# The spectral filter's products move from GpSimd to VectorE, its loads are split and issued earlier, and the planner counts the array's work differently

## The chip, the cores and the metric

The kernel runs on one core of a Trainium2 chip. The metric is the device time of one execution in microseconds. Before the change four runs took 985.72, 997.27, 997.92 and 1008.8 us; their median is 997.59 us.

## The reference

Two independent operations on 2048 x 640 inputs in bf16, whose results lie side by side in the output:

```python
# A: a spectral filter
X = jnp.fft.rfft2(x.astype(jnp.float32))       # 2048 x 321, complex
y = jnp.fft.irfft2(X * (w_r + 1j * w_i), s=(2048, 640))
# B: softmax attention, 32 heads of width 20
scores = jnp.einsum("bhqd,bhkd->bhqk", q, k) * 20 ** -0.5
o = jnp.einsum("bhqk,bhkd->bhqd", jax.nn.softmax(scores), v)
out = jnp.concatenate([y, o_merged @ wo], axis=-1)
```

## The kernel before

A planner written in Python (class `FK`) runs through an imagined execution once, at build time. It keeps a clock `self.now`, gives every operation an assumed duration, and whenever an engine would be free it picks that engine's next instruction (`dispatch`, L2188). The result is a fixed order for each of the five engines. On the chip every engine works through its list strictly in that order and waits on semaphores where data or a buffer is not ready. An instruction that has to wait holds up everything behind it on its engine. SP's list holds the DMA issues. If the imagined durations are wrong, the order stays as planned and the waits appear in the run.

*Attention.* The queries are cut into 4 blocks of 512, the heads into 8 groups of 4, which makes 32 units. A unit has 64 score tiles of 128 keys x 512 queries (16 key blocks x 4 heads). A score matmul (L1702) uses only 32 of the array's 128 rows, and up to four tiles run side by side; a PV matmul (L1884) uses 32 of the 128 columns, again four at once. ScalarE exponentiates groups of 3 and 2 tiles alternately from PSUM banks 0 to 2 and 3 to 4 (L1719). VectorE helps: it takes pairs of tiles, moves each out of PSUM (L1792) and computes the exponential in seven steps on SBUF (L1829 to L1842). At the end of a unit the sums are copied out (L1903), the denominators take a way over four small DMAs, a reciprocal (L1921), DRAM and back, and GpSimd normalizes (L1942). The output projection is L1964. Projections of keys (L1529), queries (L1605) and values (L1546, L1567) are jobs, as is everything of the filter.

*Jobs.* A `Job` is a list of matmuls into one of two PSUM banks (7 and 5) and an eviction `ev`, which any of the planner's rules may give to VectorE. The banks are shared with VectorE's score tiles. `try_bg_pe` (L2098) starts the job of the lowest priority number whose predecessors are done. Events are jobs without matmuls: they issue loads or GpSimd work and count as done after an assumed time, `lat` x 1200 ns for a load.

*The filter's stages*, as jobs with lowest precedence, one after the other:
- S2: the weights w_r and w_i are loaded (`s2_load`, L1085, two DMAs of 1284 KB), GpSimd rearranges them (`s2_relayout`, L1101), PE transposes them (L1116).
- S1: A_x is loaded (`s1_load`, L1136, one DMA of 2560 KB) and transposed (L1149). S3: DFT over columns (L1169). S4: the first factor of the DFT over rows (L1197), its constants in two loads (`s4_load`). S5: transposes (L1116).
- S6: the second factor (L1229): per chunk of 4 of 41 blocks of 128 columns two matmuls each for the real and the imaginary part, each evicted to SBUF (`XY`, by `copy_on`, L227). S7: GpSimd multiplies by the filter, six `tensor_tensor` instructions per chunk (L1258 to L1263): four products into four f32 tiles `tmp`, a difference and a sum into `XY`. The chunks go one after the other, 11 in all.
- S8 to S11: the inverse (L1229, L1116, L1297, L1323) with its constants (`s10_load`, `s11_load`).

Buffers of the stages lie over each other in zones A, B, C and K; keys such as `("z", "A", 1)` order a zone's next tenant behind the last one's readers.

*Order of the queue on PE.* `dispatch` for PE tries scores, a lone score tile for VectorE, PV, the tail, a job's next matmul, and last `warm()`, a dummy matmul (L1592). `share()` (L2169) is the planner's measure of how busy the array was over the last 2200 ns: `pe_dur` (L1634) enters every operation, 51 ns per tile for scores and PV, its duration otherwise, with 100 ns (`MODE`) where the kind of matmul changes. Dummies are placed while the share is not above `WARM_SHARE` = 0.46. Filter jobs that are ahead of a schedule, which spreads them over 680 us of planned time, are held back while the share is above it.

Of the kernel before, what the change touches and what calls it, by code (L numbers as in the profile page):

```python
# [244 lines left out]
class Job:  # L245
    def __init__(self, name, prio, pe, ev, after=(), minp=-10 ** 9, post=None, banks=None, cond=None, lat=0):
# [15 lines left out]
        self.ev_eng = None  # L262


class KB:
# [805 lines left out]
    def mk_jobs_A(self, p0_after):  # L1071
# [13 lines left out]
        def s2_load(J, p):  # L1085
            P = self.P
            wn = self.Wn
            P.add("pool", lambda e: e.memset(wn.rearrange("p c k l -> p (c k) l")[:, :, 321:328], 0.0),
                  w=zw("A", 1) + [("Wnpad",)], name="ms_wn")
            for c, src in ((0, self.A_w_r), (1, self.A_w_i)):  # L1090
                self.dma(wn[:, c, :, 0:321], src.rearrange("(kb ka) l -> ka kb l", ka=128), w=zw("A", 1) + [("Wn", c)], name="ld_W%d" % c)
            self.dma(self.kron.rearrange("p m k -> p (m k)"), self.c_kron.ap(), w=[("kron",)], name="ld_kron")
        J_s2l = evt("S2load", p0_after, s2_load, lat=8)

        J_s2r = {}
        for c in range(2):
# [6 lines left out]
            J_s2r[c] = evt("S2relayout%d" % c, [J_s2l] + ([J_s2r[0]] if c else []), s2_relayout, lat=(17 if c == 0 else 18))  # L1103
# [32 lines left out]
        def s1_load(J, p):  # L1136
            self.dma(self.xAn, self.A_x[0].rearrange("(sa sb) d -> sa sb d", sb=16), w=[("xAn",)] + zw("A", 2), name="ld_xA")
            self.dma(self.FD.rearrange("p c r l -> p (c r l)"), self.c_FD.ap(), w=[("FD",)], name="ld_FD")
        J_s1l = evt("S1load", [J_s2r[1]], s1_load, lat=8)
        st["S1"] = []  # L1140
        for dc in range(5):
            for hb in range(2):
                pe = []
                for i in range(8):
# [5 lines left out]
                    pe.append((mk, 60.0, [("xAn",), ("ident",), zr("A", 2)]))  # L1150
# [32 lines left out]
        J_s4l = evt("S4load", st["S3"], s4_load, lat=5)  # L1183
        st["S4"] = []
        for sbv in range(16):
            if sbv == 8:
                J_s4l = evt("S4load1", list(st["S4"]), lambda J, p: s4_load(J, p, 1), lat=5)
# [26 lines left out]
        def kron_jobs(tag, src, srckey, zrd, dst, dstkey, zwr, sign, after_of, stage):  # L1214
            out = {}
            for ci_, (b0, n) in enumerate(chunks):
                for co in range(2):
# [14 lines left out]
                    def mkev(bank, co=co, b0=b0, n=n):  # L1232
# [9 lines left out]
        s6 = kron_jobs("FS2_", self.BT, lambda c, ci_: ("BT", c, ci_ // 2), zr("A", 4), self.XY, lambda c, ci_: ("XY", c, ci_), zw("B", 4), +1,  # L1242
                       lambda ci_: [s5[(0, ci_ // 2)], s5[(1, ci_ // 2)]], st["S6"])
        s7 = {}
        kw = [("Wp", c, b) for c in range(2) for b in range(6)] + [zr("C", 1)]
        for ci_, (b0, n) in enumerate(chunks):
            def hook(J, p, ci_=ci_, b0=b0, n=n):
                P = self.P
                ne = n * 128
                xr = self.XY[:, 0, b0:b0 + n, :].rearrange("p b m -> p (b m)")  # L1250
                xi = self.XY[:, 1, b0:b0 + n, :].rearrange("p b m -> p (b m)")
                wr = self.Wp[:, 0, b0:b0 + n, :].rearrange("p b m -> p (b m)")
                wi = self.Wp[:, 1, b0:b0 + n, :].rearrange("p b m -> p (b m)")
                t = [tt[:, 0:ne] for tt in self.tmp]
                kx = [("XY", 0, ci_), ("XY", 1, ci_)]
                zb = [zr("B", 4)]
                tw = zw("K", 2)
                P.add("pool", lambda e: e.tensor_tensor(t[0], xr, wr, ALU.mult), r=[kx[0]] + kw + zb, w=[("tmp", 0)] + tw, name="pw")  # L1258
                P.add("pool", lambda e: e.tensor_tensor(t[1], xi, wi, ALU.mult), r=[kx[1]] + kw + zb, w=[("tmp", 1)] + tw, name="pw")
                P.add("pool", lambda e: e.tensor_tensor(t[2], xr, wi, ALU.mult), r=[kx[0]] + kw + zb, w=[("tmp", 2)] + tw, name="pw")  # L1260
                P.add("pool", lambda e: e.tensor_tensor(t[3], xi, wr, ALU.mult), r=[kx[1]] + kw + zb, w=[("tmp", 3)] + tw, name="pw")
                P.add("pool", lambda e: e.tensor_tensor(xr, t[0], t[1], ALU.subtract), r=[("tmp", 0), ("tmp", 1), zr("K", 2)], w=[kx[0]], name="pw")
                P.add("pool", lambda e: e.tensor_tensor(xi, t[2], t[3], ALU.add), r=[("tmp", 2), ("tmp", 3), zr("K", 2)], w=[kx[1]], name="pw")  # L1263
            lat = 3 + int(6 * n * 128 * 2.0 / T_PERIOD)
            aft = [s6[(ci_, 0)], s6[(ci_, 1)]] + ([s7[ci_ - 1]] if ci_ else st["S4"] + st["S2"])
            s7[ci_] = evt("S7_%d" % ci_, aft, hook, lat=lat)
# [14 lines left out]
        J_s10l = evt("S10load", [s7[nch - 1]], s10_load, lat=6)  # L1281
        st["S10"] = []
        for h in range(2):
            if h:
                J_s10l = evt("S10load1", list(st["S10"]), lambda J, p: s10_load(J, p, 1), lat=6)
# [85 lines left out]
class FK(KB):  # L1371
# [142 lines left out]
    def mk_jobs_B_static(self):  # L1514
# [5 lines left out]
        for g in range(NG):  # L1520
            for kc in range(4):
# [11 lines left out]
                if g:  # L1533
                    J.minp = 18500.0 + 1100.0 * g
        V = {}
# [98 lines left out]
    def pe_dur(self, dur, mode, tiles=0):  # L1634
        if mode != self.mode:
            dur += MODE
            self.mode = mode
        if self.now < 12000.0:
            dur *= 2.0
        self.pe_hist.append((self.now, 51.0 * tiles if tiles else dur))  # L1640
        self.wlog.append(self.pe_hist[-1])
# [435 lines left out]
    def run_events_jobs(self):  # L2077
        for J in [J for J in self.jobs if not J.pe]:
# [5 lines left out]
            if J.name.startswith("S2relayout"):  # L2084
                pool = 4600.0
            elif J.name.startswith("S7"):
                pool = 8200.0
# [279 lines left out]
```

## Time and profile before

| | before |
|---|---|
| median of 4 runs | 997.59 us |
| the profiled execution | 997.27 us, its span 995.5 us |
| PE, DVE, ACT, POOL busy | 878.4, 822.0, 848.4, 153.6 us |
| mean granted TensorE clock | 0.878 of full speed |
| ScalarE's exponentials (L1719) | 837.3 us, 724 instructions |
| VectorE's score evictions (L1792) | 163.3 us, 238 instructions of 686 ns |
| GpSimd's products (L1258 to L1263) | 66 instructions |
| dummies (L1592) | 126 |

The time lies in overlapping work of three engines, so the share of busy time says little. It is better read in stretches between two times of the span: how busy each engine was there, at which granted clock, and how many score tiles came out. The clock column is the mean of what the throttle granted in that stretch; 0.50 is half speed. A "[8.74 <-POOL arena L1101]" behind a line of the timeline means that the engine stood idle for 8.74 us before it, until that line on POOL released it. Durations of VectorE's instructions overlap their neighbours by some 0.08 us, so the distance between two starts is what one costs in a row.

### The profile page before, as it was taken

The numbers are of one execution on the slowest core, as the hardware profiler recorded it, in microseconds if no ns is written. First come the engines' busy times: TensorE is split into PE (matmuls) and PEld (weight loads), VectorE is DVE, ScalarE is ACT, GpSimd is POOL, SyncE is SP. The second block draws the span as 40 slices with busy tenths as digits, with TensorE's granted clock in tenths as the row PEclk, the third lists the DMA queues.
The fourth block names the chain that finished last, engine by engine and source line by source line (L and its number), as shares of the span: only waits on it lengthen the run. The fifth ranks groups of instructions, "written<-read, shape, count | busy, mean of one in ns | idle before, by whom it ended". The sixth has DMA issues, their size and how long they took to land.

```text
span 995.5 us, 15128 instructions
## 1 busy us (share of the span) xinstructions
PE 878.4 (88%) x6072; PEld 281.1 (28%) x6072; DVE 822.0 (83%) x1571; ACT 848.4 (85%) x744; POOL 153.6 (15%) x122
## 2 busy tenths in 40 slices
PE   8799989957999999898988878898899999898896
PEld 4333223212333332222312221332333333212212
DVE  5787999966779997879797989887899689989973
ACT  6689989975879998979968786898999899989974
POOL 4200000022000000000099653000000000010000
PEclk9899999997679998958859887797999999769959
DMA  7100000044000000110000000101101110100000
GB/s 209 34 13 12 12 6 8 12 121 151 2 19 32 13 12 12 44 33 12 13 12 15 24 13 6 50 12 54 52 12 39 39 33 33 39 12 12 12 12 29
DMA packets 31296, 31.75 MB, mean 32 GB/s; under 512 B 13300, under 2 KB 26356, under 8 KB 30836
## 3 DMA queue, kind: packets, MB, share of 16 engines
q1 hardware_dynamic: 31220, 30.73, 10.0%
q8 instruction: 49, 0.80, 0.4%
q14 instruction: 27, 0.22, 0.1%
HBM read 24.97 MB, written 5.50 MB: 31 GB/s over the span
## 4 chain that ended last, share of the span: by engine, by line
DVE 36%; PE 31%; ACT 15%; issue 7%; DMA 6%; SPq 4%; POOL 1%; ACTq 0%; POOLq 0%
ACT arena L1719 15%; PE ps L1702 10%; DVE arena L227 7%; PE ps L1884 7%; DVE arena L1792 6%; DMA arena<-arena 5%; SPq L360 4%; DVE arena L1837 4%; DVE arena L1833 3%; DVE arena L1840 3%; DVE arena L1835 3%; DVE arena L1829 3%; DVE arena L1831 2%; DVE arena L1842 2%; PE ps L1592 2%
## 5 line engine op out<-in xcount | busy, mean ns | idle before, releaser
L1719 ACT ACTIVATE arena<-ps 128x1536 bf16<-128x1536 f32 x724 | 837.3, 1261 | 125.0 <-PE ps L1702 83.5
L1702 PE MATMUL ps<-arena 32*128 32x512 bf16 x2048 | 334.9, 425 | 49.9 <-ACT arena L1719 37.6
L1884 PE MATMUL ps<-arena 128*32 128x512 bf16 (+1 forms) x2048 | 223.6, 430 | 9.4 <-DVE arena L1842 5.9
L1792 DVE TENSOR_SCALAR arena<-ps 128x512 uint16<-128x512 f32 x238 | 163.3, 686 | 46.1 <-PE ps L1702 45.2
L227 DVE CAST arena<-ps 128x320 bf16<-128x320 f32 (+5 forms) x284 | 160.8, 568 | 32.9 <-PE ps L1297 6.3
L1942 POOL TENSOR_TENSOR arena<-arena 128x512 bf16<-128x512 f32 x31 | 44.8, 1444 | 779.2 <-DMA arena<-rscr 773.2
L1702 PEld LDWEIGHTS ps<-arena 32*128 32x128 bf16 x2048 | 74.7, 92 | 271.8 <-ACT arena L1719 182.3
L1884 PEld LDWEIGHTS ps<-arena 128*32 128x32 bf16 (+1 forms) x2048 | 51.9, 93 | 152.5 <-issue 122.7
L1840 DVE TENSOR_TENSOR arena<-arena 128x1024 uint16<-128x1024 uint16 x119 | 89.3, 750 | 0.8
L1833 DVE TENSOR_TENSOR arena<-arena 128x1024 f16<-128x1024 f16 x119 | 87.1, 732 | 1.7
L1837 DVE TENSOR_TENSOR arena<-arena 128x1024 f16<-128x1024 f16 x119 | 86.7, 729 | 2.0
L1835 DVE TENSOR_SCALAR arena<-arena 128x1024 f16<-128x1024 f16 x119 | 59.8, 502 | 1.1
L1829 DVE TENSOR_SCALAR arena<-arena 128x1024 uint16<-128x1024 uint16 x119 | 59.7, 501 | 0.5
L1831 DVE TENSOR_SCALAR arena<-arena 128x1024 f16<-128x1024 int16 x119 | 57.6, 484 | 1.4
L1605 PE MATMUL ps<-arena 128*128 128x512 bf16 x160 | 55.4, 423 | 3.4 <-DVE arena L1792 2.6
L1842 DVE TENSOR_SCALAR arena<-arena 128x1024 uint16<-128x1024 uint16 x119 | 56.6, 476 | 0.5
L1592 PE MATMUL ps<-arena 128*128 128x512 bf16 x126 | 52.7, 452 | 4.7 <-DVE arena L1792 2.2
L227 DVE COPY arena<-ps 128x1024 bf16<-128x1024 bf16 (+2 forms) x54 | 33.4, 621 | 26.0 <-PE ps L1116 15.8
L1529 PE MATMUL ps<-arena 128*128 128x512 bf16 x160 | 48.6, 388 | 1.3 <-DVE arena L1792 0.7
L1116 PE MATMUL ps<-arena 128*128 128x128 bf16 x246 | 29.3, 263 | 16.9 <-POOL arena L1101 8.7
L1964 PE MATMUL ps<-arena 128*128 128x320 bf16 x192 | 39.3, 314 | 4.5 <-DVE arena L1792 2.9
L1229 PE MATMUL ps<-arena 128*128 128x512 bf16 (+1 forms) x88 | 34.5, 468 | 7.5 <-DVE arena L1792 4.0
(76 smaller groups left out, 522.5 us busy)
## 6 DMA issues: line engine op xcount, KB each, us to landing
arena<-rscr SPq DMA_DIRECT2D x31, 256.0 KB
arena<-in_B_x_dram SPq DMA_DIRECT2D x4, 640.0 KB, 6.9
arena<-in_A_x_dram SPq DMA_DIRECT2D x1, 2560.0 KB, 9.7
out_dram<-arena SPq DMA_DIRECT2D x16, 160.0 KB, 1.8
out_dram<-arena SPq DMA_DIRECT2D x4, 640.0 KB, 3.4
arena<-in_B_wqkv_dram SPq DMA_DIRECT2D x3, 700.0 KB, 9.5
arena<-f_ciCS SPq DMA_DIRECT2D x2, 1024.0 KB, 7.5
arena<-arena SPq DMA_DIRECT2D x124, 2.0 KB, 1.7
```

The lines of the kernel that those rows point to most:

```text
L227: return eng.tensor_copy(out, in_)
L1702: inst = e.matmul(ps[:, bank, :], kt_[32 * j:32 * j + 32, g, kt * 128:(kt + 1) * 128], q[32 * j:32 * j + 32, :], start=True, stop=True, ti ...
L1719: self.P.add("act", lambda e: e.activation(pt, in_, AF.Exp, scale=SCALE), r=[("ps", h + k) for k in range(n)], w=[("PT", i % 4)], name="exp")
L1792: self.P.add("dve", lambda e: e.tensor_scalar(v, in_, 1024.0 * SCALE * LOG2E, 32.0 * 1024 + 512, ALU.mult, ALU.add), r=[("ps", bank)], **( ...
L1829: t = self.x_op(n, one, lambda e: e.tensor_single_scalar(sh, v, 6, ALU.logical_shift_left), [kv], [ka], "x_s")
L1831: t = self.x_op(n, one, lambda e: e.tensor_scalar(t16, g, X_K / 65536.0, X_K * X_BETA, ALU.mult, ALU.add), [ka], [ka], "x_t")
L1833: t = self.x_op(n, two, lambda e: e.tensor_tensor(h16, t16, t16, ALU.mult), [ka], [kb], "x_q")
L1835: t = self.x_op(n, one, lambda e: e.tensor_scalar(t16, t16, X_GAMMA / X_K, 1.0 - X_GAMMA * X_BETA, ALU.mult, ALU.add), [ka], [ka], "x_l")
L1837: t = self.x_op(n, two, lambda e: e.tensor_tensor(h16, h16, t16, ALU.mult), [ka, kb], [kb], "x_h")
L1840: t = self.x_op(n, two, lambda e: e.tensor_tensor(v, v, h16, ALU.add), [kb, kv], [kv], "x_w")
L1842: t = self.x_op(n, one, lambda e: e.tensor_scalar(v, v, 0.125, X_BIAS, ALU.mult, ALU.add), [kv], [kv], "x_p")
L1884: inst = e.matmul(ps[32 * j:32 * j + m, 6, :], va[:, kt, 21 * h:21 * h + m], pt, start=st, stop=sp, tile_position=(0, 32 * j))
```

## The change

1. *Products.* The evictions of S6 and GpSimd's six instructions go. A chunk becomes two jobs: the first, for the real part, evicts by two products straight from PSUM (with w_r and w_i, into `tmp` 0 and 2); the second, for the imaginary part, by two products and then the difference and the sum into `XY`. Both are reserved for VectorE (`ev_eng`), and each waits for the one before.
2. *Loads.* The filter is loaded in eight pieces, 3 us apart in planned time, as soon as the x transposes of attention are done; the pieces no longer wait for each other. The constant `kron` is loaded behind the first relayout. A_x comes in four pieces, 4 us apart, and the constants `FD` behind them; a transpose waits only for its piece. The assumed time of the loads is raised (S2 from 8 to 32, S1 from 8 to 22, S4 from 5 to 7, S10 from 6 to 8 periods), a relayout's from 4600 to 6000 ns.
3. *Pacing.* `share()` counts streamed columns weighted by the part of the array in use, 128 per tile and 2.4 per ns otherwise, over 5280, without the time of mode changes; `WARM_SHARE` is 0.42. Key projections of group g (`soft`) are held until planned time 22000(g-1) - 4000 while the share is above it. `more_bg` lets up to three matmuls of jobs under way follow each other before PV gets its turn, as long as no more than 12 PV tiles wait.

```diff
@@ mk_jobs_A
-            for c, src in ((0, self.A_w_r), (1, self.A_w_i)):
-                self.dma(wn[:, c, :, 0:321], src.rearrange("(kb ka) l -> ka kb l", ka=128), w=zw("A", 1) + [("Wn", c)], name="ld_W%d" % c)
-            self.dma(self.kron.rearrange("p m k -> p (m k)"), self.c_kron.ap(), w=[("kron",)], name="ld_kron")
-        J_s2l = evt("S2load", p0_after, s2_load, lat=8)
+            def piece(c, k):
+                src = (self.A_w_r, self.A_w_i)[c].rearrange("(kb ka) l -> ka kb l", ka=128)
+                self.dma(wn[:, c, 4 * k:4 * k + 4, 0:321], src[:, 4 * k:4 * k + 4, :], r=[zr("A", 0)], pw=[("Wn", c)], name="ld_W%d" % c)
+            for i in range(8):
+                self.at(self.now + 3000.0 * i, lambda i=i: piece(i // 4, i % 4))
+        J_s2l = evt("S2load", [j for j in p0_after if j.name[0] == "x"], s2_load, lat=32)
...
+                if c:
+                    self.dma(self.kron.rearrange("p m k -> p (m k)"), self.c_kron.ap(), w=[("kron",)], name="ld_kron")
+            J_s2r[c] = evt("S2relayout%d" % c, ([J_s2r[0]] if c else [J_s2l] + p0_after), s2_relayout)
...
-            self.dma(self.xAn, self.A_x[0].rearrange("(sa sb) d -> sa sb d", sb=16), w=[("xAn",)] + zw("A", 2), name="ld_xA")
-            self.dma(self.FD.rearrange("p c r l -> p (c r l)"), self.c_FD.ap(), w=[("FD",)], name="ld_FD")
-        J_s1l = evt("S1load", [J_s2r[1]], s1_load, lat=8)
+            def piece(k):
+                self.dma(self.xAn[:, 4 * k:4 * k + 4, :], xa[:, 4 * k:4 * k + 4, :], w=[("xAn", k)], pw=zw("A", 2), name="ld_xA")
+            for k in range(4):
+                self.at(self.now + 4000.0 * k, lambda k=k: piece(k))
+            self.at(self.now + 16000.0, lambda: self.dma(self.FD.rearrange("p c r l -> p (c r l)"), self.c_FD.ap(), w=[("FD",)], name="ld_FD"))
+        J_s1l = evt("S1load", [J_s2r[1]], s1_load, lat=22)
...
-                P.add("pool", lambda e: e.tensor_tensor(t[0], xr, wr, ALU.mult), r=[kx[0]] + kw + zb, w=[("tmp", 0)] + tw, name="pw")
...
+            def mult(k, w, ne=ne, t=t):
+                def mkev(bank):
+                    return lambda e, en: e.tensor_tensor(t[k], ps[:, bank, 0:ne], w, ALU.mult)
+                return (mkev, 0.0, 1.0417 * ne + 64, kw, [("tmp", k)] + zw("K", 2), [])
...
+                if co == 0:
+                    ev = [mult(0, wr), mult(2, wi)]
+                    aft = [s5[(0, ci_ // 2)], s5[(1, ci_ // 2)]] + ([s7[ci_ - 1]] if ci_ else st["S4"] + st["S2"])
+                else:
+                    ev = [mult(1, wi), mult(3, wr), comb(y0, 0, 1, ALU.subtract, ("XY", 0, ci_)), comb(y1, 2, 3, ALU.add, ("XY", 1, ci_))]
+                    aft = [s7[ci_]]
+                s7[ci_] = self.add_job(Job("FS2_%d_%d" % (ci_, co), PRIO, pe, ev, after=aft))
+                s7[ci_].ev_eng = "dve"
@@ mk_jobs_B_static
+                J.soft = 22000.0 * (g - 1) - 4000.0
@@ pe_dur
+        self.pe_hist.append((self.now, 128.0 * tiles if tiles else 2.4 * dur))
+        self.wlog.append(self.pe_hist[-1])
         if mode != self.mode:
             dur += MODE
...
-        self.pe_hist.append((self.now, 51.0 * tiles if tiles else dur))
@@ try_bg_pe
+        elif self.now < J.soft and self.share() > self.cfg["WARM_SHARE"]:
+            return False
...
+    def more_bg(self):
+        if self.mode != "f" or self.f_run >= self.cfg["RUN"] or not self.att or self.u_pv >= 32:
+            return False
+        if len(self.pv_ready[self.u_pv]) > self.cfg["PVQ"]:
+            return False
+        for J in self.inflight:
+            if J.nxt < len(J.pe):
+                self.bg_chunk(J)
+                return True
+        return False
@@ share
-        return sum(d for _, d in h) / 2200.0
+        return sum(d for _, d in h) / 5280.0
@@ dispatch
-            return (self.try_qk() or self.try_x_alone() or self.try_pv(4) or self.tail_pe() or self.try_bg_pe() or self.warm())
+            return (self.try_qk() or self.try_x_alone() or self.more_bg() or self.try_pv(4) or self.tail_pe() or self.try_bg_pe() or self.warm())
@@ the call
-    fast = FK(nc, arena, *args, cfg=dict(LEAD=20, T_A=680000.0, WARM_SHARE=0.46))
+    fast = FK(nc, arena, *args, cfg=dict(LEAD=20, T_A=680000.0, WARM_SHARE=0.42, RUN=3, PVQ=12))
```

## The prediction

> **What bounds the kernel now.** I read the windows by stage first, because busy shares over the whole span (PE 88%, ACT 85%, DVE 83%) name no bound. The work that fixes the end is 2048 score tiles. ScalarE exponentiates most of them in instructions of 3 or 2 tiles (362 of each, so 2.5 on average), and VectorE does the rest in 119 pairs. I cut the span where the filter's stages change; columns are PE, PEld, DVE, ACT, POOL busy, then granted clock.
> ```profile
> 200.00:300.00 100.00, 78.98 (x578) 29.37 (x578) 70.88 (x134) 73.19 (x64) 12.86 (x5) 0.76 0.22 73
> 300.00:400.00 100.00, 92.09 (x676) 30.42 (x673) 90.56 (x193) 93.39 (x82) 5.24 (x4) 0.97 0.06 17
> 400.00:490.00 90.00, 82.98 (x544) 23.58 (x542) 75.33 (x155) 79.37 (x69) 4.72 (x3) 0.77 0.09 28
> 490.00:612.00 122.00, 102.31 (x603) 26.89 (x603) 105.59 (x146) 93.82 (x82) 86.26 (x69) 0.80 0.04 13
> 612.00:720.00 108.00, 96.84 (x696) 32.56 (x696) 88.08 (x168) 96.32 (x84) 5.49 (x4) 0.86 0.13 39
> 720.00:850.00 130.00, 119.27 (x891) 42.25 (x890) 111.61 (x234) 121.31 (x106) 5.54 (x4) 0.98 0.11 36
> 850.00:975.00 125.00, 111.02 (x672) 26.06 (x668) 107.14 (x215) 112.61 (x97) 8.29 (x5) 0.79 0.04 12
> ```
> Tiles finished are 2.5 times the ACT count plus twice the pairs (L1840 in the same windows: 10, 16, 11, 10, 11, 19, 22). From 720 to 850 that is 106 x 2.5 + 38 = 303 tiles in 130 us, 2.33 per us; 300 to 400 gives 2.37. Against 2.33 the others fall behind: 200 to 300 makes 180 tiles and loses 100 - 180/2.33 = 22.7 us; 490 to 612 makes 225 and loses 25.4; 400 to 490 loses 6.5, 612 to 720 8.4, 850 to 975 2.0. These are the sums that the change can win from.
>
> In the first bad stage I read the timeline.
> ```profile
> 201.14 0.42 SPq L360 DMA_DIRECT2D arena<-in_A_w_r_dram  x1
> 209.03 0.38 SPq L360 DMA_DIRECT2D arena<-in_A_w_i_dram  x1
> 211.38 0.57 SPq L360 DMA_DIRECT2D arena<-rscr  x1
> 218.51 1.26 POOL L1942 TENSOR_TENSOR arena<-arena 128x512 bf16<-128x512 f32 x1 [37.58 <-DMA arena<-rscr]
> 219.72 9.18 POOL L1101 COPY arena<-arena 128x5248 bf16<-128x5248 bf16 x2
> 224.42 1.01 PE L1116 MATMUL ps<-arena 128*128 128x128 bf16 x8 [8.74 <-POOL arena L1101]
> 226.02 2.54 ACT L1719 ACTIVATE arena<-ps 128x1536 bf16<-128x1536 f32 x2 [8.52 <-PE ps L1702]
> 226.08 3.10 DVE L1835 TENSOR_SCALAR arena<-arena 128x1024 f16<-128x1024 f16 x1
> ```
> The second filter load waits for the first, SP's queue stands, the normalization's read (211.38) is late, POOL's relayout starts behind it, and PE, which takes its queue in order, stops at the transposes of its result. Everything else stops with it. The 2.6 MB of A_x then arrive behind that, PE stops again (2.11 and 1.85 us busy in 235 to 240 and 240 to 245), and the clock is 0.50 from 240 to 265.
>
> In 490 to 612 POOL computes the filter products. VectorE's groups in this window against 720 to 850 show what that does.
> ```profile
> L1831 DVE TENSOR_SCALAR arena<-arena 128x1024 f16<-128x1024 int16 x9 | 10.8, 1200 | 0.1
> L1829 DVE TENSOR_SCALAR arena<-arena 128x1024 uint16<-128x1024 uint16 x9 | 9.0, 1001 | 0.1
> L1842 DVE TENSOR_SCALAR arena<-arena 128x1024 uint16<-128x1024 uint16 x10 | 8.9, 888 | 0.0
> ```
> The same three take 423, 423 and 469 ns from 720 to 850. Over the seven steps of the exponential the excess is 7.0 + 5.2 + 4.2 + 3.8 (L1835) + 3.6 (L1833) + 3.5 (L1840) + 2.7 (L1837) = 30.0 us of VectorE spent blocked.
>
> Third, the clock. Cut into 2 us windows, it is below 0.6 in 212 us; ACT is busy 66% there and 96% where it is above 0.95 (60 to 960 us). One cold microsecond so costs 1 - 66/96 = 0.31 us.
>
> **The change part by part.** Filter products. A plane has 41 x 128 = 5248 columns, 10.25 full chunks. Removed: 66 POOL instructions (mean 1163 to 1340 ns, 83.5 us), the 30.0 us of blocking, and two evictions per chunk. Added on DVE: six instructions per chunk for those two. Four read PSUM: nearest rows L1792 and L1903, 128x512 f32, which show 0.68 us but start 0.60 apart back to back, so 0.60 is the price. Two combine f32 tiles in SBUF: nearest row L1833, a two-input instruction over as many bytes, also 0.60 apart. Net four more: 4 x 10.25 x 0.60 = 24.6 us. No row has a two-input read of PSUM; bounds per instruction 0.33 (half the bytes) and 1.3 (the blocked L1831), which would make it 11 to 60 us; I keep 24.6. What it displaces: a pair takes two evictions and three two-input steps at 0.60 and four at 0.34 = 4.4 us, so 5.6 pairs, 11 tiles, 4.8 us at 2.33. Recoverable: 25.4 - 4.8 = 20.6. Not all: a chunk's second job puts four instructions, 2.4 us, ahead of score evictions and the PV copy L1903 in VectorE's order, and each chunk waits for the one before. I take two thirds, 14 us.
>
> Loads. Eight filter pieces after the x transposes (the last ends at 40.0 us), at a time when W has 160 us to spare. They drop the write-after-write wait (SP's 7.5 us) and the 9 us landing. What POOL has to do ahead of them, a 285 ns memset, falls where POOL is empty (30 to 64.7). A_x goes in four pieces of some 2.5 us each. SP issues 9 more DMAs at 0.33 to 0.57 us, about 4 us; its queue waits 448 us for L1903 anyway. Behind those issues stand the denominators (first at 54.19) and the output weights, first used at 284: one piece in front of a denominator costs VectorE's L1921 at most some 2.5 us, once or twice. The kron load moves past POOL's first relayout; its first use is at 493. SP still waits for the relayouts before A_x, and the relayouts (9.1 us) still block VectorE's steps, as L1835's 3.10 us shows. The planner's 6.0 us for a relayout, against 4.56 measured, places PE's transposes later, after their data. Longer load allowances for the constants (about 2.4 us each, and some 17 for A_x) delay filter jobs, with scores or dummies in between; without that cover each costs its own length. I take three quarters of 22.7: 17 us.
>
> Pacing. The old rule counts 51 per tile, matmul time otherwise, and 100 ns per mode change into a dense run. From 850 to 975, where only pacing rules, there are 576 tile matmuls and 96 dense ones in 71 runs: (576 x 51 + 96 x 216 + 71 x 100)/125000 = 0.458, the old 0.46. By the new count the same queue is (576 x 128 + 96 x 512)/(125 x 2400) = 0.41; the new floor is 0.42. So the floor rises by 0.01, some 7 dummies in 81. Keeping up to three dense matmuls of a job together saves mode changes (0.1 us each) on a PE that has slack when warm. Here a rule of the Trainium skill speaks against any gain. First the row:
> ```profile
> 425.00:430.00 5.00, 4.95 (x23) 0.50 0.02 3
> 430.00:435.00 5.00, 5.00 (x23) 0.50 0.16 23
> 435.00:440.00 5.00, 5.00 (x27) 0.50 0.36 134
> 440.00:445.00 5.00, 5.00 (x24) 0.50 0.01 0
> ```
> PE is busy throughout and stays at half clock. "TensorE: Matmul & The Clock Gate", Part 1, says that the array is warm again after about 3.4 us of sustained busy time. By that, dips heal themselves and pacing is worth 0: sum 31, 966 us. The trace says busy is not enough: 74 quarter-array tiles and 23 dense matmuls in those 20 us (7 of 512 columns, 16 of 328) are 0.38 of full-speed work. So what is queued matters; but since the floor hardly moves I take a quarter of 6.5 + 8.4 + 2.0: 4 us.
>
> Key projections held until 22(g-1) - 4 us: the last one ran at 199 before, its hold ends at 128; units end 28 us apart (L1903), so none is late. Filling of the start is unchanged: 0, between -4 and +4.
>
> Sum: 14 + 17 + 4 = 35 us from the profiled execution's 997.3 (span 995.5 and 1.8 around it), 962; the median, 997.6, is the same.
>
> **The rivals.** (a) Only the loads pay: VectorE becomes the filter stage's bound, its chunks a chain of products, evictions and late scores, and 490 to 612 stays as slow as now. For it: VectorE is at 105.6 of 122 us there. Against: 30 of those are blocking. 997 - 17 = 980. (b) Everything recovers, the cold stretches too: 20.6 + 22.7 + 17 = 60, 937. Against: nothing feeds the array much more. (c) Slower: the share no longer counts mode changes, dense jobs bunch, and the gaps between bunches fall under the clock's need. Price 0.31 per cold microsecond. To pass 1017 it must eat the 31 us of the other two parts and 20 more: 51/0.31 = 165 us more cold, about a doubling of what lies after 300. Then 1018, with the filter stage cold as well 1030. The point is where activity in a paced stage drops from 0.41 to under the 0.38 that stayed cold: not far. (d) The planner's order comes out no better: new waits of the same kind (L1921 waits 38.1 us for denominators, untouched) replace the old: 990.
>
> **How the numbers follow.** Forecast (950 to 972) 0.52; (b) 0.14; (a) 0.16; (d) 0.10; (c) 0.08. Range 938 to 990: it leaves out (c), half of (d) and the edge of (b). A measurement of this kernel tells about 2% from no change (runs before: 985.7 to 1008.8), here 978 to 1018. Faster: forecast, (b) and a third of (a), 0.71; same: the rest of (a) and (d), 0.21; slower 0.08.
>
> **What would show it.** No POOL products, and L1829 to L1842 back at their 720 to 850 means in the filter stage; PE's 8.7 us wait for L1101 gone and W landing before 80 us; filter stage shorter than 85 us; dummies (126) about as many; clock mean up from 0.878 to 0.90 or more. Wrong if the new products start 1 us apart, if PE waits for them by more than 15 us in all, or if the clock stays at 0.88.

## The result and the profile after

The changed kernel takes 978.5 us (median of 12 runs, 968.5 to 1012.3) against 997.5 us (17 runs, 985.7 to 1019.0) for the one before. The ratio is 0.983, with a 95% interval of 0.979 to 0.987; it is taken over the executions within 1.5% of their kernel's fastest, while the medians, here and below, are of all executions. The forecast was 962 us and a gain of 35; 19 came. The direction is right, the time is inside the range of 938 to 990, and the gain is about half.

The page of the changed kernel first: busy times, then the span in 40 slices.

```profile
span 976.8 us, 15047 instructions
PE 860.6 (88%) x6045; PEld 275.7 (28%) x6045; DVE 834.3 (85%) x1633; ACT 845.1 (87%) x743; POOL 72.8 (7%) x56
ACT  5789988797889898999888687579999899999984
POOL 4200000220000000000000000000000000000000
PEclk9999999896779899999778586779998799999979
```

POOL lost 81 us of work (153.6 before), and VectorE is only 12 us busier. In the rows, counted from 0, POOL's block in slices 20 to 24 is gone. But the clock still has its two dips, at slices 9 to 11 (behind the second relayout) and 19 to 27 (filter), and ACT dips where the clock does. The mean clock rose from 0.878 to 0.897; 0.90 or more was named.

The windows by stage, cut where the stages of this kernel change (columns: PE, PEld, DVE, ACT, POOL busy, granted clock, DMA share, GB/s):

```profile
200.00:300.00 100.00, 87.37 (x645) 31.04 (x643) 80.48 (x150) 84.23 (x74) 9.30 (x4) 0.81 0.16 47
300.00:400.00 100.00, 89.30 (x657) 28.72 (x653) 86.00 (x180) 92.02 (x82) 5.29 (x4) 0.95 0.06 17
400.00:490.00 90.00, 79.62 (x564) 22.86 (x561) 84.62 (x179) 85.71 (x75) 4.02 (x3) 0.92 0.09 28
545.00:652.00 107.00, 90.11 (x462) 19.80 (x462) 90.77 (x161) 79.67 (x69) 4.04 (x3) 0.72 0.06 18
652.00:750.00 98.00, 86.19 (x697) 30.55 (x697) 86.40 (x168) 96.42 (x85) 5.19 (x3) 0.98 0.09 31
```

In 200 to 300 ACT is 84 us busy (73 before), a gain, though not the recovery of a stage that works at full rate. S6 to S8 now run from 545 to 652: 107 us, at a clock of 0.72, with ACT at 74%. That stage was to be shorter than 85 us.

*The load stage.* The timeline at the first relayout:

```profile
181.92 5.05 POOL L1104 COPY arena<-arena 128x5248 bf16<-128x5248 bf16 x1
183.06 4.19 DVE L1857 TENSOR_SCALAR arena<-arena 128x1024 f16<-128x1024 f16 x1
189.18 1.46 PE L1546 MATMUL ps<-arena 128*128 128x512 bf16 x3 [3.90 <-DVE arena L227]
191.23 1.45 ACT L1741 ACTIVATE arena<-ps 128x1536 bf16<-128x1536 f32 x1 [4.17 <-PE ps L1724]
```

The loads did what they were meant to: the last piece is issued at 58.7 us, and PE's 8.74 us wait for POOL is gone. A different stall stands there now. A VectorE step that takes 0.42 us elsewhere takes 4.19: it starts during GpSimd's copy (181.92 to 186.97) and ends just after it. (With shorter copies the steps beside them are shorter too, see below.) The evictions behind it are late, PE waits 3.90 us for one of them, and ACT 4.17 us for PE. Then the clock falls: it is below 0.6 from 188 to 198, and again from 220 to 236 after the second relayout at 216.4.

*The filter stage.* The new products, by shape (groups of the changed kernel; count, then busy us and mean ns):

```profile
L1262 DVE TENSOR_TENSOR arena<-ps,arena 128x512 f32<-128x512 f32 x40 | 27.6, 690 | 7.8 <-PE ps L1274 6.8
L1267 DVE TENSOR_TENSOR arena<-arena 128x512 bf16<-128x512 f32 x20 | 14.7, 734 | 0.3
L1857 DVE TENSOR_SCALAR arena<-arena 128x1024 f16<-128x1024 f16 x7 | 3.9, 550 | 0.0
L1853 DVE TENSOR_SCALAR arena<-arena 128x1024 f16<-128x1024 int16 x6 | 2.4, 422 | 0.1
```

The last column is the idle time before them: of the products' 7.8 us, 6.8 end with L1274. L1853 (L1831 before) is back at 422 ns from the 1200 it took beside GpSimd's products. In the timeline below two of them take 1.32 us from start to start, 0.66 each, so the price of 0.60 for a two-input read of PSUM was close. And VectorE makes only 7 pairs of score tiles in these 107 us: the filter takes its time.

```profile
629.86 1.41 DVE L1262 TENSOR_TENSOR arena<-ps,arena 128x512 f32<-128x512 f32 x2
631.18 1.41 DVE L1267 TENSOR_TENSOR arena<-arena 128x512 bf16<-128x512 f32 x2
632.50 0.69 DVE L227 CAST arena<-ps 128x512 bf16<-128x512 f32 x1
633.25 1.04 PE L1274 MATMUL ps<-arena 128*128 128x512 bf16 x2 [2.65 <-DVE arena L227]
637.43 4.65 ACT L1741 ACTIVATE arena<-ps 128x1024 bf16<-128x1024 f32 x4 [9.96 <-PE ps L1906]
```

Here VectorE works through a chunk without a gap (2.7 us for two products and two combinations), and the next filter matmul, in a bank that the eviction L227 must first empty, waits 2.65 us at the head of PE's queue. The PV matmuls (L1906 on PE) stand behind it and its neighbours, and one of them is what releases ACT, idle for 9.96 us. ACT did not lack scores: it starts at 637.43 on scores that were there by 628.6, as the next score matmul comes at 638.70. In the program PV frees for ACT a buffer of exponentials, which ACT writes and PV reads.

### The profile page after: what moved, and what is told of

Its sections match the earlier page's. It is cut to its first block, busy times and chain, and to the rows that moved or that the text cites. A ratio compares the mean times of both kernels' runs of the same rounds, so it can differ in the third digit from the quotient of the medians.

```text
span 976.8 us, 15047 instructions
## 1 busy us (share of the span) xinstructions
PE 860.6 (88%) x6045; PEld 275.7 (28%) x6045; DVE 834.3 (85%) x1633; ACT 845.1 (87%) x743; POOL 72.8 (7%) x56
## 3 DMA queue, kind: packets, MB, share of 16 engines
q1 hardware_dynamic: 31748, 30.73, 10.7%
## 4 chain that ended last, share of the span: by engine, by line
DVE 42%; PE 29%; ACT 16%; DMA 5%; SPq 4%; issue 2%; ACTq 0%; DVEq 0%
ACT arena L1741 16%; PE ps L1724 9%; DVE arena L1814 7%; DVE arena L227 7%; PE ps L1906 6%; DMA arena<-arena 5%; SPq L361 4%; DVE arena L1855 4%; DVE arena L1859 4%; DVE arena L1862 3%; DVE arena L1857 3%; DVE arena L1851 3%; DVE arena L1864 3%; DVE arena L1853 2%; PE ps L1623 2%
## 5 line engine op out<-in xcount | busy, mean ns | idle before, releaser
L1724 PE MATMUL ps<-arena 32*128 32x512 bf16 x2048 | 329.1, 414 | 55.6 <-ACT arena L1741 42.0
L1906 PE MATMUL ps<-arena 128*32 128x512 bf16 (+1 forms) x2048 | 219.9, 422 | 10.8 <-DVE arena L1864 8.4
L1814 DVE TENSOR_SCALAR arena<-ps 128x512 uint16<-128x512 f32 x242 | 165.9, 686 | 36.3 <-PE ps L1724 35.2
L227 DVE CAST arena<-ps 128x320 bf16<-128x320 f32 (+4 forms) x262 | 146.8, 561 | 27.9 <-PE ps L1623 4.6
L1906 PEld LDWEIGHTS ps<-arena 128*32 128x32 bf16 (+1 forms) x2048 | 52.0, 93 | 152.8 <-issue 112.2
L1862 DVE TENSOR_TENSOR arena<-arena 128x1024 uint16<-128x1024 uint16 x121 | 86.5, 715 | 0.7
L1855 DVE TENSOR_TENSOR arena<-arena 128x1024 f16<-128x1024 f16 x121 | 83.8, 693 | 1.7
L1859 DVE TENSOR_TENSOR arena<-arena 128x1024 f16<-128x1024 f16 x121 | 83.6, 691 | 1.6
L1857 DVE TENSOR_SCALAR arena<-arena 128x1024 f16<-128x1024 f16 x121 | 59.1, 488 | 1.1
L1623 PE MATMUL ps<-arena 128*128 128x512 bf16 x160 | 54.5, 422 | 1.8 <-DVE arena L1814 1.8
L1853 DVE TENSOR_SCALAR arena<-arena 128x1024 f16<-128x1024 int16 x121 | 52.8, 437 | 1.2
L1546 PE MATMUL ps<-arena 128*128 128x512 bf16 x160 | 48.6, 401 | 5.5 <-DVE arena L227 4.6
L227 DVE COPY arena<-ps 128x1024 bf16<-128x1024 bf16 (+2 forms) x54 | 33.4, 621 | 17.5 <-PE ps L539 8.0
L1340 PE MATMUL ps<-arena 128*128 128x320 bf16 (+1 forms) x192 | 41.8, 319 | 2.4 <-DVE arena L1814 1.4
L1610 PE MATMUL ps<-arena 128*128 128x512 bf16 x99 | 38.0, 413 | 5.8 <-DVE arena L1814 4.7
L1179 PE MATMUL ps<-arena 128*128 128x328 bf16 x160 | 35.6, 323 | 2.0 <-DVE arena L1814 1.6
```

The source lines that it names most:

```text
L227: return eng.tensor_copy(out, in_)
L1623: return lambda e: e.matmul(o, l, r_, start=st, stop=sp)
L1724: inst = e.matmul(ps[:, bank, :], kt_[32 * j:32 * j + 32, g, kt * 128:(kt + 1) * 128], q[32 * j:32 * j + 32, :], start=True, stop=True, ti ...
L1814: self.P.add("dve", lambda e: e.tensor_scalar(v, in_, 1024.0 * SCALE * LOG2E, 32.0 * 1024 + 512, ALU.mult, ALU.add), r=[("ps", bank)], **( ...
L1855: t = self.x_op(n, two, lambda e: e.tensor_tensor(h16, t16, t16, ALU.mult), [ka], [kb], "x_q")
L1857: t = self.x_op(n, one, lambda e: e.tensor_scalar(t16, t16, X_GAMMA / X_K, 1.0 - X_GAMMA * X_BETA, ALU.mult, ALU.add), [ka], [ka], "x_l")
```

## The experiments

**One part alone, and the order redrawn.** Each of three kernels has one part of the change on the kernel before: the loads (the hunks of `s2_load`, the relayout, S1, S4 and S10), the products (S6 and S7), the pacing (`share`, `soft`, `more_bg`, weights). The fourth is the kernel before with one planner constant altered, the assumed delay from a TensorE instruction to what depends on it:

```diff
-PE_LAT = 170.0
+PE_LAT = 172.0
```

It does nearly the same work in another order. The order also settles who takes a tile, and where dummies go: VectorE takes 236 score tiles instead of 238.

> The kernel before with the loads' part alone (pieces, early filter, raised load and relayout allowances). The prediction's sums say -17 us (ratio 0.983) and PE's 8.7 us wait for the relayout gone. Rival read off the trace after: the two relayouts still block VectorE for 4 us each and the array goes cold behind them, so tiles in the load stage rise by under 10 and the ratio is 0.995 or more.

> The kernel before with the products on VectorE alone. The prediction says -14 us (0.986). Rival: the blocking is gone but a chunk still takes 9 to 10 us, because the stage runs at half clock and VectorE's products stand before the score evictions; then 0.995 to 1.005, with cold time in the filter stage as long as before.

> The kernel before with the new share, threshold 0.42, held key projections and runs of up to three dense matmuls. The prediction says -4 us (0.996). Rival read off the trace after, where tiles were gained from 400 to 475 and from 650 to 975: pacing carries most of the gain, 0.985 to 0.99, with less cold time after 300 us.

> The kernel before with only the planner's assumed latency of a matmul's result raised from 170 to 172 ns: the same work in another order (some thousand lines of PE's list differ). If a new order by itself moves the time, the ratio lies as far from 1 as those of the parts, 1% or more; if order is worth little, within 0.5% of 1.

Measured: loads 978.4 us, products 986.1, pacing 1002.3 (ratio 0.994 to 1.006), the redrawn order 972.1 (ratio 0.964, 0.952 to 0.976). The last is the finding of the study: altering nothing but the order wins 25 us by the medians (four executions, 964 to 1006) and 3.6% by the ratio, more than the change wins. So no single pair of kernels says what a part is worth. The medians of this study are of 4 to 17 executions, which spread over 10 to 44 us within one kernel; the kernel before, measured again beside each group, had medians of 996.6 to 1000.1. The row of clocks of the redrawn kernel shows what goes with it:

```profile
PEclk9899999997899999979978666999999899689997
```

Its two dips are shorter than in before: 140 us lie below a clock of 0.6, against 212.

**The changed kernel redrawn, and three edits inside its order.** The next four are built on the changed kernel. The first has `PE_LAT` 172. The others keep its order: GpSimd's relayout in seven pieces of up to six blocks instead of one copy; 88 further dense matmuls in the filter's jobs, whose results are overwritten; and the difference and the sum computed on 16 columns only, so that the filter's product is left incomplete.

```diff
@@ relayout_in_pieces
-                P.add("pool", lambda e: e.tensor_copy(o, i_), ...)
+                for b0 in range(0, 41, 6):
+                    def f(e, b0=b0):
+                        return e.tensor_copy(o[:, b0:min(b0 + 6, 41)], i_[:, b0:min(b0 + 6, 41)])
+                    P.add("pool", f, ...)
@@ denser_filter
+        if J.nxt == 0 and J.name.startswith(("FS2_", "IS2_")):
+            for _ in range(2):
+                self.P.add("pe", mk(J.bank, x=True), r=rk, w=[key], name=J.name + ".extra")
...
@@ sums_cut
-                    return lambda e, en: e.tensor_tensor(y, t[k0], t[k1], op)
+                    return lambda e, en: e.tensor_tensor(y[:, 0:16], t[k0][:, 0:16], t[k1][:, 0:16], op)
```

> The changed kernel with only the planner's assumed matmul latency raised from 170 to 172 ns, as in before_reshuffled. If the change as a whole is worth 2%, its second order lies 2% under the mean of the two orders of before (998 and 972): near 966. If the order decides and the change little, it may lie anywhere from 965 to 1000, and with both orders counted change and before overlap.

> The changed kernel, every engine's order kept, but each of GpSimd's two relayouts issued as seven copies of 6 blocks (0.7 us each) in place of one of 4.9 us. If GpSimd's lock on VectorE is what still costs the load stage (VectorE's 4.19 and 4.06 us steps, ACT 4.2 and 3.0 us idle behind them and cold stretches of 12 and 18 us), those steps fall under 1.5 us, the cold stretches shrink and the time falls by 6 to 10 us, to about 970. If the stage is limited by its loads or by the order anyway, no change within 3 us.

> The changed kernel, every engine's order kept, but the first matmul of each of the 44 jobs of the two kron stages is issued three times into the same bank (the first two as matmuls of their own that are overwritten): 88 more dense matmuls, 19 us of array work at full clock. If the stage from 545 to 645 is slow because the array is cold for lack of dense work, its clock rises from 0.7 to above 0.85 and the kernel gets 5 to 15 us faster in spite of the added work. If VectorE's order is the bound, the time stays or rises by up to 19 us.

> The changed kernel, every engine's order kept, but the difference and the sum of each chunk run over 16 of its columns only, so the filter's product is left incomplete: VectorE has 22 x 0.5 = 11 us less in the filter stage. If VectorE's time and order bound that stage, it shortens by 8 to 11 us and the kernel with it; if the cold array bounds it, by under 4.

Measured: 978.8, 979.3, 986.9 and 978.0 us. None is distinguishable from the 978.5 of the changed kernel; even the removal of 11.5 us of VectorE's work in the filter stage (the 22 combinations are busy 3.8 us instead of 15.3) is not. The reason can be followed in the traces, since with one order the count of score tiles says directly how far ahead one kernel is. With the cut sums the kernel is 36 score matmuls ahead of the changed one at 650 us (1354 against 1318, some 15 us; 9 of them at 545, as its filter starts 3 us earlier) and 12 ahead at 900. Its windows, then those of the changed kernel:

```profile
700.00:750.00 50.00, 44.46 (x297) 13.67 (x296) 43.62 (x88) 44.50 (x40) 3.75 (x2) 0.85 0.10 32
750.00:775.00 25.00, 25.00 (x127) 6.78 (x123) 16.09 (x34) 17.12 (x15) 0.00 (x0) 0.56 0.05 15
```

```profile
700.00:750.00 50.00, 42.77 (x328) 13.69 (x327) 47.77 (x94) 49.44 (x44) 3.62 (x2) 1.00 0.13 48
750.00:775.00 25.00, 24.26 (x136) 6.90 (x135) 19.41 (x41) 18.93 (x17) 1.27 (x1) 0.66 0.05 18
```

The first is the kernel that was ahead. It stays at half clock from 735 to 772, the other from 751 to 768. In the kernel with the denser filter the time below 0.6 between 500 and 700 falls from 80 to 38 us, as meant, and it is given back at the end:

```profile
930.00:970.00 40.00, 38.34 (x178) 8.26 (x179) 25.92 (x51) 29.75 (x26) 1.27 (x1) 0.50 0.03 8
```

Forty microseconds at half clock, PE busy 96% of them, where the changed kernel has 0.84.

The filter stage itself tells two of the edits apart. Here it is with the sums cut, then with the denser filter; the changed kernel's own line, 545 to 652, stands further up:

```profile
542.00:637.00 95.00, 76.28 (x458) 19.47 (x465) 78.52 (x163) 77.44 (x69) 3.81 (x3) 0.86 0.07 21
547.00:655.00 108.00, 91.21 (x538) 27.01 (x546) 89.39 (x161) 79.23 (x68) 3.92 (x3) 0.90 0.06 18
```

For about as many score tiles (180 in the changed kernel, 180 and 183 here), the stage takes 95 us instead of 107 when VectorE has 11.5 us less to do. With the clock at 0.90 instead of 0.72 it still takes 108. So in this order VectorE's work seems to set the stage's length more than the half clock does. That rests on one execution each, and the 88 added matmuls take time of their own, so what the warm clock alone would give is not shown.

With the relayout in pieces VectorE's steps (L1857 and L1861, here two lines later than above) are blocked for a moment only:

```profile
187.53 1.17 DVE L1857 TENSOR_TENSOR arena<-arena 128x1024 f16<-128x1024 f16 x1
190.56 1.30 DVE L1861 TENSOR_TENSOR arena<-arena 128x1024 f16<-128x1024 f16 x1
193.48 1.03 PE L1548 MATMUL ps<-arena 128*128 128x512 bf16 x2 [2.54 <-DVE arena L227]
```

These two take 0.69 us elsewhere, and the seven copies take 6.8 us in all; the longest step beside either relayout takes 1.37 us, against 4.19, and PE waits 2.54 us instead of 3.90. The end does not come sooner.

A gain in one stage shifts everything behind it, and in these traces other stretches then fall to half clock. This also happens between executions of one and the same order: the 12 runs of the changed kernel go from 968.5 us at a mean clock of 0.910 to 1012.3 at 0.851.

**More draws.** So both kernels were redrawn twice more, with `PE_LAT` 168 and 174.

> The kernel before with the planner's TensorE latency at 168 instead of 170: the same work in another order (as 172 was, which gave 972 against 998). Theory A (the change itself is worth about 1.7%, and the 972 was one lucky order): this kernel lies near before's 998, and the changed kernel with 168 lies some 15 to 20 us under it. Theory B (a draw of the order moves the time by some per cent either way, by which stretches of background work fall into the half clock; before's own order was a poor draw): this kernel lies anywhere in 970 to 1000, with its time rising about 0.3 us for each us below a clock of 0.6 in its trace.

> The changed kernel with 168 instead of 170. Theory A: 975 to 982, and 15 to 20 us under before_168. Theory B: 970 to 990, and its difference from before_168 has either sign, as it had with 172 (978.8 against 972.1).

> The kernel before with 174. Theory A: near 998. Theory B: anywhere in 970 to 1000, following the time its trace spends below a clock of 0.6.

> The changed kernel with 174. Theory A: 975 to 982, and 15 to 20 us under before_174. Theory B: 970 to 990, and of the four pairs (168, 170, 172, 174) at least one more besides 172 shows the change within 8 us of nothing or slower.

| `PE_LAT` | 168 | 170 | 172 | 174 | mean |
|---|---|---|---|---|---|
| before | 978.7 | 997.5 | 972.1 | 976.7 | 981.2 |
| changed | 959.6 | 978.5 | 978.8 | 954.4 | 967.8 |
| difference | -19.1 | -19.0 | +6.7 | -22.4 | -13.4 |

Neither of the two theories holds as it was put: before with 168 is not near 998, and no further pair beside 172 showed the change at nothing. The change gains in three of four orders; with 172 it shows no gain, and four executions a side are too few to call it a loss. The mean, -13.4, has a standard error of some 7 us, so four orders make a gain likely and do not settle its size. The order in which the kernel before was given is its worst of the four. Its four orders scatter by 11 us (standard deviation), the changed kernel's by 13. The changed kernel with 174 is the best of all that ran, 954.4 us, ratio 0.952 (0.945 to 0.960) to the kernel before as given; against its own pair, 976.7, the medians give 0.977. In the two quick orders of the changed kernel (168 and 174) VectorE also takes 234 score tiles instead of 242 and 240; what that does was not tried by itself. The row of clocks of the changed kernel with 174 has one shallow dip where the relayouts are, and shorter ones after:

```profile
PEclk9999998979999999889988769999977999988669
```

**Each part in three orders.**

> Only the early loads in pieces, on the kernel before with 168 (978.7). If the parts keep the proportions of the prediction (17 of 35 for the loads) and the whole is worth 19 to 22 us here: 967 to 971. If the loads are worth what the first 400 us of the first comparison showed (about 4 us): 973 to 977. If a draw of the order outweighs each part: anywhere in 955 to 990, and not adding up with the other two parts.

> Only the early loads in pieces, with 174 (before 976.7, whole change 954.4). Proportions of the prediction: 965 to 969. Loads worth about 4 us: 971 to 975. Draw of the order: anywhere in 955 to 990.

> Only the products on VectorE from PSUM, on the kernel before with 168 (978.7). Proportions of the prediction (14 of 35): 969 to 973. If the filter stays at half clock and its jobs alternate with VectorE, so that the products are worth nothing by themselves: 976 to 981. Draw of the order: anywhere in 955 to 990.

> Only the products on VectorE from PSUM, with 174 (before 976.7). Proportions of the prediction: 967 to 971. Products worth nothing by themselves: 974 to 979. Draw of the order: anywhere in 955 to 990.

> Only the pacing (weights, three background matmuls in a row, soft due times), on the kernel before with 168 (978.7). Proportions of the prediction: 975 to 978. Nothing, as at 170: 976 to 984. If it is what the other two parts leave over of the whole at this order (960 for all three, loads +1 and products -11 alone): 967 to 972. Draw of the order: anywhere in 955 to 1000.

> Only the pacing, with 174 (before 976.7). Proportions of the prediction: 973 to 976. Nothing, as at 170: 974 to 982. If it is what the other two parts leave over of the whole at this order (954 for all three, loads -3 and products -11 alone): 966 to 971. Draw of the order: anywhere in 955 to 1000.

Medians, and the difference from the kernel before of the same order:

| part alone | 168 | 170 | 174 | mean difference | forecast |
|---|---|---|---|---|---|
| loads | 979.8 (+1.1) | 978.4 (-19.1) | 973.4 (-3.4) | -7 | -17 |
| products | 968.0 (-10.7) | 986.1 (-11.4) | 966.0 (-10.8) | -11 | -14 |
| pacing | 974.7 (-4.0) | 1002.3 (+4.8) | 980.4 (+3.7) | +2 | -4 |
| all three | 959.6 (-19.1) | 978.5 (-19.0) | 954.4 (-22.4) | -20 | -35 |

With a scatter of 11 us per order, a mean of three differences is known to about 9 us only, so these means do not size the parts. The 172 order, in which the whole change shows no gain, is not among them, as the parts were not run in it. The traces size the parts better, stage by stage. Count the time that a stage takes and subtract what the score matmuls begun in it would have taken at 2.4 per us, the rate of the good stretches (the five best of the changed kernel have 120 to 126 in 50 us). For the stage from the first matmul of S6 to the last of S8, from the profiled executions, in us lost:

| S6 to S8 | 168 | 170 | 172 | 174 |
|---|---|---|---|---|
| before | 37.8 | 31.1 | 37.3 | 35.2 |
| loads alone | 30.4 | 37.2 | | 29.0 |
| pacing alone | 38.0 | 37.8 | | 39.8 |
| products alone | 28.1 | 21.9 | | 29.2 |
| all three | 19.7 | 32.1 | 29.8 | 25.0 |

Without the new products (the first three rows) the mean is 35.4, with them 26.5. The products win 9 us in their own stage, with a standard error of 2. The changed kernel itself has the 32.1, the worst of its seven. The same account for the load stage, from 50 us to the last matmul of S3:

| 50 us to S3 | 168 | 170 | 172 | 174 |
|---|---|---|---|---|
| before | 22.7 | 36.0 | 28.5 | 24.2 |
| products alone | 18.7 | 38.0 | | 35.4 |
| pacing alone | 31.7 | 29.6 | | 22.8 |
| loads alone | 21.3 | 22.5 | | 23.5 |
| all three | 26.9 | 35.5 | 28.6 | 21.7 |

Without the early loads the mean is 28.8, with them 25.7. The loads win 3 us there, with a standard error of 3. Together that is 12, against 13.4 for the mean difference over four orders.

For the given pair (170) the two tables say something else. Neither stage gained: 31.1 against 32.1, and 36.0 against 35.5. Of the 19 us, 17 come from the stretch between the end of S8 and the last score matmul, which lost 21.5 us before and 4.2 after. Of the change only the pacing and the longer allowance for S10's constants act in it. Its windows before, after, and in the kernel before with 172, which has none of the change and loses 0.6 there:

```profile
627.00:977.00 350.00, 316.14 (x2175) 97.94 (x2173) 293.15 (x588) 319.35 (x277) 18.70 (x13) 0.87 0.08 26
652.00:959.00 307.00, 273.10 (x2008) 87.17 (x2008) 277.99 (x556) 291.11 (x254) 16.70 (x11) 0.94 0.09 28
608.00:949.00 341.00, 295.34 (x2207) 95.37 (x2230) 303.91 (x619) 324.97 (x285) 24.96 (x13) 0.95 0.09 30
```

The clock is 0.87, 0.94 and 0.95. So the 19 us of this pair are not the two parts at work; they come with a warmer end, which the order alone also gives. Over all 17 kernels this stretch loses 9 us with the pacing and 12 without (standard error 3), and 12 with the loads' part and 10 without.

Why so little for the loads? The kernel before with 168, which lost only 22.7 us there, has the old loads, but not the stall. Its POOL timeline:

```profile
189.53 4.77 POOL L1101 COPY arena<-arena 128x5248 bf16<-128x5248 bf16 x1 [7.94 <-DMA arena<-in_A_w_r_dram]
217.24 4.75 POOL L1101 COPY arena<-arena 128x5248 bf16<-128x5248 bf16 x1
```

POOL waits 7.94 us for the load, and PE does not wait for POOL. In this order the old loads start at 181.6 instead of 201.1, the first relayout is over at 194.3, and the transposes begin at 217.8, much as in the changed kernel (relayouts at 181.9 and 216.4). PE's longest waits here are 3.31 and 3.52 us, for VectorE's blocked step and for an eviction behind one, as in the changed kernel. With 172 and 174 the old stall is there (PE waits 8.1 and 8.3 us for POOL), and yet those orders lose 28.5 and 24.2 us, not 36. What the loss in this stage follows is the time at half clock in it: over the 17 kernels the two rise together, from 10 us cold and 18.7 lost to 58 cold and 38.0 lost (correlation 0.87; which is the cause is not shown by that).

## Why the prediction was half right

*What held.* POOL's products are gone. VectorE's integer steps take 420 ns again in the filter stage. The new products start 0.66 us apart against the 0.60 assumed. PE waited 0.5 us in all for the products themselves, and the matmuls that feed them (L1274) 8.3 us, mostly for the eviction L227, under the 15 named. W is in place by 65 us, and PE's 8.7 us wait has vanished. The product term, 14 us, measured 9 in its stage and 11 over three orders: right in mechanism and somewhat too high. PE's queue now waits for VectorE in that stage (2.65 us in the timeline above), and cutting VectorE's sums shortened the stage by 12 us. In the given pair the term did not show at all (31.1 lost before, 32.1 after). The bounds of 11 to 60 us that the prediction sets beside its 24.6 do not follow from its formula, which gives 14 and 53 for 0.33 and 1.3 us; nothing rests on them.

*The step that failed: "three quarters of 22.7: 17 us" for the loads.* It measured 3 us in its stage and 7 over three orders. Two things are wrong in it. First, the 22.7 us were read from one order as if they belonged to the late loads. In the order drawn with 168 the same loads cost no stall on PE, and with 172 and 174 the stall was there and the stage lost 8 to 12 us less. Only with 170 did the loads alone win something like the forecast, 13.5 us in their stage and 19 in all; with 168 and 174 it was 1 us in the stage. Secondly, the prediction saw that the relayouts "still block VectorE's steps" and set no price on it. That blocking, 4 us for each relayout, then stops PE and ACT as the load wait had, and the clock falls behind it. The dip was moved from 224 to 188 and 220. Yet this is not shown to be worth much by itself: in seven pieces no step of VectorE beside it takes more than 1.37 us, and the time was 979.3 us. What makes the cold stretches long stays open.

*Luck.* The time fell into the range, but not as forecast: in this pair the 19 us came after S8, where the forecast had put at most its pacing term, and an order of the kernel before does as well there.

*The pacing term*, 4 us, has not been seen: -4.0, +4.8 and +3.7. "About as many" dummies was wrong too: 99 for 126. In the changed kernel one lies between 525 and 650, where the clock is lowest.

*The rule of the Trainium skill that was set aside* ("TensorE: Matmul & The Clock Gate", Part 1: warm after some 3.4 us of sustained busy time) stays contradicted, if busy means what the profile counts as busy. With the sums cut, PE is busy for all of 750 to 775 and at half clock for 21 of these 25 us (window further up). There, as in the prediction's own case, most matmuls use a quarter of the array (71 of 99 from 751 to 772). The windows of the changed kernel before and in its filter stage are close to it:

```profile
525.00:550.00 25.00, 23.11 (x126) 6.50 (x125) 19.03 (x39) 16.89 (x15) 1.27 (x1) 0.59 0.08 25
550.00:575.00 25.00, 21.65 (x106) 4.43 (x105) 20.35 (x37) 18.24 (x16) 1.27 (x1) 0.66 0.04 11
```

PE is 90% busy over 50 us and has 0.59 and 0.66. What was taken from the rule, that pacing would be worth nothing, came true all the same, but not for the rule's reason, as the dips did not heal.

*The rivals.* (a), 980 us, came nearest by its time. In this pair the filter stage did stay as slow as (a) has it; over the orders its mechanism is the wrong way round: the products paid, and the loads hardly did. (b), with the cold stretches recovered, did not occur. (d), new waits in place of old, is what happened in the load stage. (c) did not occur. The price of a cold microsecond, estimated at 0.31 us from ACT's share, agrees with a count that does not use ACT, though a slope does not show which is the cause: over 20 kernels of this study, the profiled span rises by 0.30 us for each microsecond below a clock of 0.6 (correlation 0.79; 134 to 236 us cold, 957 to 996 us of span).

*What no case of the prediction contained* is that the order itself is a draw worth some 11 us either way. A range for a kernel with a planned order should carry that from the start.

Still open: what chooses the stretches that go cold from one execution to the next, why 172 shows no gain, and whether the three parts gain more together (20) than their sum (17), which lies within the scatter.

## What to carry to other kernels

Where a planner writes the order, redraw the order before believing a comparison: two or three settings of a constant without meaning give the scatter, and their best may beat the change under test. Size a part by what its own stage loses, over several orders, rather than by the end-to-end time of one pair. Ask also whether the gain lies in the stage that was changed: here most of it did not. And before pricing a stall as recoverable, ask what stands behind it: here the copy that follows the load stops the same engines.

## What was not expected of the hardware

- Half clock lasted 40 us in one piece (930 to 970, above) with PE 96% busy, though at 178 matmuls in 40 us, most of which (146) use a quarter of the array; and 21 us with PE busy throughout (751 to 772 with the sums cut).
- One order, 12 executions: 968.5 to 1012.3 us, with the mean granted clock from 0.910 down to 0.851, about 7 us for each 0.01.
- A VectorE product that reads one f32 operand from PSUM and one bf16 operand from SBUF (128x512) takes 0.69 us and 0.66 from start to start, about what a plain eviction of that shape takes (L227: 0.69).
